# Two attention layers and two linear-attention layers on one core: 27 normalised rows to GpSimd, more PSUM homes, a new order

## The chip, the core and the metric

The kernel runs on one core of a Trainium2 chip. It uses TensorE (matmul; PE in the profile), VectorE (DVE), ScalarE (ACT), GpSimd (POOL) and the queues of SyncE (SP) and ScalarE for transfers. The metric is the device time of one execution in microseconds, as the median of several runs.

## The reference

The input X has 2048 rows (tokens) of 512 numbers, in bfloat16. Four blocks follow each other, A, B, A, B, and each adds its result to X:

```
x = x + A(layernorm(x))
x = x + B(layernorm(x))
x = x + A(layernorm(x))
x = x + B(layernorm(x))
layernorm(x) = (x - mean) / sqrt(var + 1e-5)      # per row
```

A is attention with 32 heads of 16 numbers in four segments of 512 tokens. Within a segment it is causal softmax attention. From the second segment on a memory is added: the sum of phi(k) v over the earlier segments, read with phi(q), with phi(t) = t + 1 above zero and exp(t) below. A gate per head mixes the two. B is linear attention without a mask: q and k go through a small matrix per head, a softmax of the result and one of its negative make the features, the sum of features of k times v is taken over all tokens, and q reads it. Both end with a projection.

## The kernel before

X stays in SBUF as 16 tiles of 128 tokens. A chunk is four tiles, which is also a segment of A. The work of the two layers (L = 0 and 1, each one A and one B) is cut into steps. A step is what one engine does without a wait in between, and it belongs to one of these families (names as in the code, line of the profile behind them):

- **ln** (lines 790 to 825) normalises a chunk: per tile `stats` (L801) and `aggr` (L802) on VectorE, `veps` (L811) and `pow` (L813) for 1/sqrt, then `xn` (L817): (X - mean) times 1/sqrt, one tile of 128 x 512 in bfloat16, 64 of them in the program, all on VectorE. Two tiles make a pair, which one DMA transposition (L585) on SP's queue turns into `xA`, `EQ` or `xB`. Some tiles stand alone; those are turned by TensorE (L601) and copied out of PSUM by VectorE or ScalarE.
- **a_proj** makes k, q and v of a segment. Results come in a PSUM bank and are copied out (L579, tiles `ktok`, `QT`, `VT`); `lo` (L907, L908) is a shifted copy of half a tile of `xA`, `kp` (L938, L939) a copy of parts of K.
- **a_att** does the attention. A unit is two score steps, one on each half of TensorE's rows, each with 1024 columns in two PSUM banks (a *score pair* of banks, kind `st`). ScalarE takes the exponential of such a pair in one instruction (`exp`, L1104, 288 of them), into a tile `PT`. Units on the diagonal are masked: `mask.odd` (L1110) on VectorE or GpSimd, `mask.even` (L1113) on GpSimd. Then TensorE multiplies with v (`pv`, into one bank), and VectorE divides (`r1` L1138, `norm` L1139).
- **a_mem**, **a_state** hold the memory; **a_out** projects, and `resid` (L1165) or `resid.act` (L579, tile `X`) adds to X.
- **b_keys** takes exponentials (L1200), sums them (`bk.half` L1207 on GpSimd, `bk.sum` L1209), inverts (L1218), writes a column of `Vt` (`bk.z`, L1220 to L1222) and the scaled v (L1228). **b_queries** and **b_out** read the sum. `bq.wide` (L1304) widens a 128 x 32 tile on ScalarE or GpSimd.

The order of all this is not made by loops. The program lists 3416 steps with their dependences; four tables at the head of the file then say how they run (`replay`, line 353):

- `ORDER` lists the steps in one sequence. Each engine's queue is its part of that sequence. A number over 10000 marks a score step whose matmuls are issued alternately with those of the step before it (67 of them), so that both halves of TensorE's rows work at once. A negative number is a filler: so many matmuls on a tile of zeros (L1431) where TensorE would have nothing to do (33 fillers with 129 matmuls).
- `ENGINE` has one letter for each step that several engines may run (568 of them), in the order of their creation.
- `SLOTS` gives each tile its buffer, and each PSUM result its bank or banks, as a place in the list of its kind.
- `AFTER` lists pairs of steps (126), the first of which also waits for the second. All 126 are a GpSimd step that waits for a VectorE step.

The kinds of PSUM results and their banks, at line 664:

```
"st": [(0, 1), (2, 3), (4, 5)],
"pv": [(7,), (6,), (5,), (4,)],
"gen": [(7,), (6,), (5,), (4,)],
```

`gen` is a single bank, for projections and the like (289 results), `st` a score pair (288), `pv` the product with v (72). A step of a kind that may run on VectorE or GpSimd is made by `either` (line 575).

Of the kernel before, what the change touches and what calls it, by code (L numbers as in the profile page):

```python
# [8 lines left out]
ALU = mybir.AluOpType  # L9
# [266 lines left out]
class Program:  # L276
# [22 lines left out]
    def R(self, *key):  # L299
        r = self.fixed.get(key)  # L300
        if r is None:
            r = self.fixed[key] = Res()
        return r
# [236 lines left out]
class Kernel:  # L540
# [249 lines left out]
    def ln(self, c, pris, groups=((0, 1), (2, 3)), by_pe=(), pool=None, by_act=False):  # L790

        R = self.R
# [683 lines left out]
```

## Time and profile before

| | |
|---|---|
| median of 3 runs | 478.36 us (478.14 to 478.48) |
| profiled execution | 478.63 us |
| span of its trace | 476.9 us |
| granted TensorE clock | 1.00 |
| HBM read, written | 6.32 MB, 2.10 MB |

The span is from the first to the last instruction of the profiled execution; the 1.7 us between it and that execution's time lie outside it. Busy times are the union of an engine's instructions. PE is TensorE's matmuls, whose ends are modelled; PEld is its weight loads. A row of a group reads: line, engine, operation, tile written <- tiles read, shapes, count | busy us, mean ns of one | idle us of the engine just before them and who ended it.

### The profile page before, as it was taken

The numbers are of one execution on the slowest core, as the hardware profiler recorded it, in microseconds if no ns is written. First come the engines' busy times: TensorE is split into PE (matmuls) and PEld (weight loads), VectorE is DVE, ScalarE is ACT, GpSimd is POOL, SyncE is SP. The second block draws the span as 40 slices with busy tenths as digits, with TensorE's granted clock in tenths as the row PEclk, the third lists the DMA queues.
The fourth block names the chain that finished last, engine by engine and source line by source line (L and its number), as shares of the span: only waits on it lengthen the run. The fifth ranks groups of instructions, "written<-read, shape, count | busy, mean of one in ns | idle before, by whom it ended". The sixth has DMA issues, their size and how long they took to land.

```text
span 476.9 us, 19206 instructions
## 1 busy us (share of the span) xinstructions
PE 465.2 (98%) x8309; PEld 319.3 (67%) x8309; DVE 424.0 (89%) x1008; ACT 429.7 (90%) x666; POOL 268.9 (56%) x435
## 2 busy tenths in 40 slices
PE   7999999999999999999999999999999999999997
PEld 6786677567756567557687666766765666665763
DVE  6999899989998988688999999999998888978885
ACT  3989999999999999986799899989999999999742
POOL 3686758656756685510267575784677578761100
DMA  8679661342422132320346417155434121313366
GB/s 264 115 202 147 144 92 25 69 69 47 48 46 47 25 65 51 36 55 4 67 62 97 74 21 134 25 75 83 59 63 63 25 47 33 51 38 58 70 128 186
DMA packets 115091, 35.86 MB, mean 75 GB/s; under 512 B 106816, under 2 KB 115008, under 8 KB 115008
## 3 DMA queue, kind: packets, MB, share of 16 engines
q1 hardware_dynamic: 112608, 32.54, 38.3%
q10 hardware_dynamic: 2400, 2.11, 1.4%
q8 instruction: 65, 1.06, 0.9%
q14 instruction: 18, 0.15, 0.1%
HBM read 6.32 MB, written 2.10 MB: 18 GB/s over the span
## 4 chain that ended last, share of the span: by engine, by line
PE 59%; DVE 18%; ACT 17%; DMA 3%; POOL 2%; issue 1%; POOLq 0%; DVEq 0%
PE PS L520 57%; ACT PT L1104 12%; DVE D L1110 2%; DVE stats L801 2%; DVE Vt L1228 2%; ACT Ek L1200 2%; DVE xn L817 1%; PE PS L601 1%; DMA EQ<-xn 1%; PE PS L1431 1%; DMA OT<-O 1%; DVE O L1139 1%; ACT K L1285 1%; DVE X L1165 1%; DVE Zk L1209 1%
## 5 line engine op out<-in xcount | busy, mean ns | idle before, releaser
L1104 ACT ACTIVATE PT<-PS 128x1024 bf16<-128x1024 f32 x288 | 284.6, 1083 | 7.8 <-PE PS L520 7.5
L1110 POOL TENSOR_TENSOR D<-PT,modd 128x256 bf16<-128x256 bf16 x133 | 91.6, 699 | 54.2 <-ACT PT L1104 39.1
L1113 POOL TENSOR_SCALAR_AFFINE_SELECT PT<-PT 128x512 bf16<-128x512 bf16 x128 | 83.9, 664 | 30.8 <-DVE D L1110 27.4
L520 PEld LDWEIGHTS PS<-VT,PT 128*128 128x128 bf16 x2048 | 75.0, 96 | 19.2 <-POOL PT L1113 2.5
L520 PE MATMUL PS<-VT,PT 128*128 128x17 bf16 x2048 | 82.4, 171 | 0.7 <-POOL PT L1113 0.2
L520 PE MATMUL PS<-QT,K 32*128 32x64 bf16 (+2 forms) x2176 | 77.9, 213 | 0.3
L520 PE MATMUL PS<-VT,D 128*128 128x17 bf16 x512 | 59.9, 170 | 0.0
L520 PEld LDWEIGHTS PS<-QT,K 32*128 32x128 bf16 x2176 | 41.5, 93 | 20.6 <-ACT PT L1104 10.5
L1110 DVE TENSOR_TENSOR D<-PT,modd 128x256 bf16<-128x256 bf16 x123 | 42.9, 362 | 2.9 <-ACT PT L1104 1.5
L520 PEld LDWEIGHTS PS<-VT,D 128*128 128x128 bf16 x512 | 43.2, 96 | 0.0
L1228 DVE TENSOR_TENSOR Vt<-PS,Zk 128x1024 bf16<-128x1024 f32 (+1 forms) x34 | 39.0, 1158 | 2.0 <-PE PS L520 1.0
L801 DVE BATCH_NORM_STATS2 stats<-X 128x6 f32<-128x512 bf16 x56 | 37.3, 681 | 2.5 <-DMA X<-in_A_x_dram 2.2
L1200 ACT ACTIVATE Ek<-PS 128x512 bf16<-128x512 f32 x64 | 37.6, 664 | 0.9 <-PE PS L520 0.9
L520 PE MATMUL PS<-WA_v,xA 128*128 128x256 bf16 x256 | 36.6, 273 | 0.1
L520 PE MATMUL PS<-WA_k,xA 128*128 128x256 bf16 x256 | 36.3, 273 | 0.2 <-POOL xA L907 0.2
L520 PE MATMUL PS<-xA,WA_q 128*128 128x128 bf16 x512 | 35.7, 219 | 0.5 <-DVE MS L986 0.2
L1165 DVE TENSOR_TENSOR X<-X,PS 128x512 bf16<-128x512 bf16 x50 | 33.7, 679 | 2.2 <-PE PS L520 1.8
L1207 POOL TENSOR_TENSOR Vt<-Ek 128x512 f32<-128x512 bf16 x24 | 27.9, 1164 | 12.9 <-ACT Ek L1200 10.4
L520 PEld LDWEIGHTS PS<-xA,WA_q 128*128 128x128 bf16 x512 | 29.8, 98 | 4.6 <-issue 0.6
L520 PE MATMUL PS<-WA_o,OT 128*128 128x512 bf16 x128 | 32.0, 380 | 0.6 <-DMA OT<-O 0.4
L520 PE MATMUL PS<-WB_o,OT 128*128 128x512 bf16 x128 | 32.1, 379 | 0.1
L1304 POOL COPY O<-rho 128x512 bf16<-128x512 bf16 x24 | 14.9, 634 | 26.5 <-DVE rho L1297 23.3
(157 smaller groups left out, 980.7 us busy)
## 6 DMA issues: line engine op xcount, KB each, us to landing
X<-in_A_x_dram SPq DMA_DIRECT2D x3, 512.0 KB, 9.9
EQ<-in_B_wqkv_dram SPq DMA_DIRECT2D x2, 512.0 KB, 5.4
out_dram<-X SPq DMA_DIRECT2D x8, 128.0 KB, 2.0
out_dram<-X ACTq DMA_DIRECT2D x8, 128.0 KB, 1.9
OT<-O SPq DMA_TRANSPOSE x42, 3.2
WB_v<-in_B_wqkv_dram SPq DMA_DIRECT2D x1, 512.0 KB, 4.3
WA_o<-in_A_wo_dram SPq DMA_DIRECT2D x1, 512.0 KB, 6.5
WB_o<-in_B_wo_dram SPq DMA_DIRECT2D x1, 512.0 KB, 4.7
```

The lines of the kernel that those rows point to most:

```text
L520: return e.matmul(o, l, r, start=st, stop=sp, tile_position=(basep(l), basep(o)))
L601: ins = e.transpose(self.bank(gen).bitcast(BF16)[:, dt * 128:(dt + 1) * 128], src()[:, dt * 128:(dt + 1) * 128], self.ident[:])
L801: self.dve(lambda e, t=t, src=src: e.bn_stats(self.stats[:, t, :], src()), 0.603, [held() if held else R("X", t)], [R("stats", t)], name=" ...
L817: self.dve(lambda e, t=t, n=n, xn=xn: e.tensor_scalar(xn.ap[:, n], self.X[:, t, :], self.mv[:, t, 0:1], self.rstd[:, t:t + 1], op0=ALU.sub ...
L1104: self.act(lambda e, st=st, pt=pt: e.activation(pt.ap[:].rearrange("p b c -> p (b c)"), self.ps[:, st.slot[0] * 512:st.slot[0] * 512 + 102 ...
L1110: self.either(lambda e, d=d, k=k, pt=pt: e.tensor_tensor(d.ap[:, :, k, :].rearrange("p b (z c) -> p b z c", z=2), self.ends(pt.ap[:, :, 25 ...
L1113: self.pool(lambda e, q=quarters: e.affine_select(q(), q(), [[0, 4], [1, 128]], ALU.is_ge, 0.0, base=0, channel_multiplier=-1), 0.6, [pt() ...
L1165: self.dve(lambda e: e.tensor_tensor(X[:, t, :], X[:, t, :], self.bank(gen), ALU.add), 0.6, [R("X", t), gen()], [R("X", t)], name="resid")
L1200: self.act(lambda e, sgn=sgn, Ek=Ek, gen=gen: e.activation(Ek.ap[:, sgn, :], self.bank(gen), ACT.Exp, scale=1.0 - 2.0 * sgn), 512, [gen()] ...
L1207: self.pool(lambda e, Ek=Ek, sums=sums: e.tensor_tensor(sums(), *(Ek.ap[:].rearrange("p s (h j) -> p s h j", h=H)[:, :, :, 8 * k:8 * k + 8 ...
L1228: self.dve(lambda e, w=w, n=n, Vt=Vt, Zk=Zk, gen2=gen2: e.tensor_tensor(self.signed(Vt)[:, w, :, 0:16], self.bank(gen2).rearrange("p (h d) ...
L1304: P.add(("act", "pool"), {"act": lambda e, dst=dst, src=src: e.activation(dst(), src(), ACT.Copy), "pool": lambda e, dst=dst, src=src: e.t ...
```

## The change

Three edits, and new tables.

1. `xn` is made by `either`, so that each of the 64 rows has a letter in `ENGINE` (632 letters).
2. Score pairs may also lie in banks 6 and 7, and single results (`gen`) also in banks 3 and 2.
3. `ORDER`, `AFTER`, `ENGINE` and `SLOTS` are new throughout.

```diff
@@ -31,179 +31,181 @@
 ORDER = (
...
 )
 AFTER = (
-    (389, 128), (164, 47), (181, 51), (353, 38), (371, 144), (201, 191), (212, 152), (202, 192), (213, 175), (1142, 370), (260, 43), (261, 154),
...
+    (91, 88), (169, 351), (341, 1140), (77, 1138), (389, 112), (170, 746), (353, 50), (186, 51), (165, 1139), (197, 196), (1142, 192), (213, 212),
...
 )
@@ -663,9 +665,9 @@
         self.PS.kinds = {
-            "st": [(0, 1), (2, 3), (4, 5)],
+            "st": [(0, 1), (2, 3), (4, 5), (6, 7)],
             "pv": [(7,), (6,), (5,), (4,)],
-            "gen": [(7,), (6,), (5,), (4,)],
+            "gen": [(7,), (6,), (5,), (4,), (3,), (2,)],
             "two": [(6, 7), (4, 5), (0, 1), (2, 3)],
             "wide": [(7,), (6,), (4,), (5,), (0,), (1,), (2,), (3,)],
         }
@@ -814,9 +816,9 @@
             xn = self.p_xn.tile()
             for n, t in enumerate(4 * c + i for i in grp):
-                self.dve(lambda e, t=t, n=n, xn=xn: e.tensor_scalar(xn.ap[:, n], self.X[:, t, :], self.mv[:, t, 0:1], self.rstd[:, t:t + 1],
-                                                                    op0=ALU.subtract, op1=ALU.mult), 0.324,
-                         [R("X", t), R("mv", t), R("rstd", t)], [xn(n)], port=True, name="xn")
+                self.either(lambda e, t=t, n=n, xn=xn: e.tensor_scalar(xn.ap[:, n], self.X[:, t, :], self.mv[:, t, 0:1], self.rstd[:, t:t + 1],
+                                                                       op0=ALU.subtract, op1=ALU.mult), 0.324, 0.63,
+                            [R("X", t), R("mv", t), R("rstd", t)], [xn(n)], name="xn")
```

The tables, read out step by step, say the following. Counts of steps per engine that differ:

| step | VectorE | ScalarE | GpSimd |
|---|---|---|---|
| xn | 64 to 37 | | 0 to 27 |
| mask.odd | 123 to 126 | | 133 to 130 |
| copy of k (`ktok`) | 10 to 15 | 18 to 13 | |
| copy of v (`VT`) | 15 to 16 | 17 to 16 | |
| resid.act (`X`) | 2 to 4 | 6 to 4 of those that may move | |
| turned rows (`xA`) | 3 to 5 | 5 to 3 | |
| kp | 13 to 15 | 2 to 3 | 17 to 14 |
| lo | 11 to 10 | 6 to 6 | 15 to 16 |
| bk.z | 7 to 6 | 4 to 9 | 21 to 17 |
| bq.wide | | 8 to 6 | 24 to 26 |
| folded weight (`WB`) | 7 to 6 | 1 to 2 | |
| turned output (`OT`) | 7 to 6 | 5 to 6 | |

The rows moved to GpSimd belong to 20 pairs and 2 tiles that stand alone: in 15 pairs one row of the two moves, in 5 both. Score steps that are issued alternately with the one before go from 67 to 75, fillers from 33 with 129 matmuls to 36 with 143, entries of AFTER from 126 to 142, each again a GpSimd step that waits for a VectorE step. Stores from ScalarE's queue go from 8 to 7, from SP's from 8 to 9.

| PSUM results | banks 0/1 | 2/3 | 4/5 | 6/7 |
|---|---|---|---|---|
| score pairs (288) | 132 to 132 | 137 to 97 | 19 to 33 | 0 to 26 |
| single results `gen` (289) | 0 | 0 to 68 | 128 to 109 | 161 to 112 |

More of the change, by code (lines that the diff above doesn't have):

```diff
@@ L33 @@
 ORDER = (
[137 rows of a table removed]
[137 rows of a table added]
 )
 AFTER = (
[12 rows of a table removed]
[14 rows of a table added]
 )
 ENGINE = (
-    "daddaadadaadadapaapapadaadaapppddppddpdpdpddpdpdpppppdppddpdpapadpadadpdpdapapaddaddddddppppapapppdppdpdddddppdpdddpdppppdddpppddpddadpaadad"
-    "daaddadddpdapdpppappdpdddddpppdpppdddddddppdpddddppddpddpapaapadaadaddapdpdddpppppppdppddppdddddddddddppdppddddddpddpdpppddadappdpappadaaaaa"
-    "aaaaaadaaapdapdadpaddddddpadaapppppdpdddppddddpdppppdpdppdpddpdadddpdpadaaaadpapadpdppapppddppppppddddpppdddppppppdppddpppppdddapaapaaaapddd"
-    "apapaadpappppppdddddddppdpddpddddppppdppppddddpppdddddddaddaadpaddapddadppppppdpdppppddddpdppdddpdpppddddddpdpppddpddaddpdaapapaasasassasaaa"
@@ L191 @@
-    "aassdads"
+    "dddaddddaaddpdapadapaapddaaaadaadpdpppdpddddddddpdpdppppddppppdpppddpadadpapadpdaddpapaadadddddadddppappapppddpppdpppdppddddddddddppppppdddd"
+    "pppddpdppdddaaadddddpaaddddadpdppapppppppdpppddpdppddpdpddpdddppdddddpdppdddpdpppapaadadaapadddpddaddddddadppppppddpddpppddddddpdddppdpppddd"
+    "dppdpdppdddadddddapddpapppaddaaaadpadadddddaaapaapdaaaaddddaddddaadddpdpppdpdddddddpppppddddppddppdpppdaaddpddadpapadaapddpddpadppapapdppppp"
+    "ppddddpppdddpddpdpdpppdppppddddpdpaapaapapaaddpaaadpdadpdppppappppppdpdpddppdddddddddpddpppdppdppdpdddpppppddddddpdddddadpdddddpddpdaapppppd"
@@ L192 @@
+    "pppppppddpdppddddpdpdppddddppdddddpddadppdddpaappapaasaasssassassasadaaa"
 )
 SLOTS = (
-    "00001102030001020030111201203100120141131150261033007081111329031012001000001131231051221312013312002300037180012120111134021610039001002130"
-    "01301102006021210004019120120031231700001313001120208101100011002711900231111104062201100210203305170010310221130013100381901022313032110310"
-    "00611111004022202331120212233150810310330312020700210328190100113105100210013320710109030231118000012015013000221710100121300113410112503711"
@@ L197 @@
-    "02000131800100202110123003261901201312103415013100021170111220023360211232800913010031310120022170009111051038001011000309011223100037021110"
-    "22025081100302001137190111100003031516031002020021201320040381113112001322130351200161012220133000112323319012303101107120221121214003518000"
-    "10230209031200102001061030271013120411100301052193686272072110202112210012430006121012023333123245167302013210120314500040153201305112300161"
-    "07025123011123210110311001214710050002241011500023203160311110128091001200030710032235022110111124061003011313230028101022101139100021224102"
@@ L201 @@
-    "71001123061101231210021002901113034081031200110310410160212311013017081021010121011000235061213031090101220213000001210310303041002001332210"
-    "35061121322700110238100324130190101001120122210103303001104120171001121001121309100131011030002103204110022117081111200300012011229110020103"
-    "24100300611112280030029131000110212101050710122026101119001310003211713221801112142021035012133222718033119101021314002231112017100503081090"
-    "01113270302024013210518011011000210406110321110700102313203103212109041210320601110001703123213100230301519022112330122218033061123210123506"
@@ L205 @@
-    "13210239011020070113182300001002214130200311501611200122321031023711110008954301673041113200050231103211074036521000721210010314300013412512"
-    "1130101130043156211207122130021306451"
+    "00100102034050000001111220011304100213115061207021030101458092510210102103001023105121112200133413001210819300231031002121060112030137102110"
+    "00213020040233106003107120300041520328000411010022005119000114021708211330104261110200221010230042135370115403103101201200381901230123200103"
+    "10401211126102002311021210233519012133003071020231003081900010021031050213201170110381023021309113110110170100201801132103205111100003113023"
@@ new lines @@
+    "26010401518310040353432030709352302011120304036111103308110122011002122003270110233115091122312073480501330341001010051220801217210900113011"
+    "02102304103025121080911030013341521307320305320433202035250631113011002102113120030271203311101042159240010312400082530100212232150103061201"
+    "01320204091300102301170000228103201051021104126379201121180211030412252502430110030252412330323241506172010223110024534005011670046512172300"
+    "11057221102602214032115030243400103213518020131306073063201110273901504000350381120002111340110023100602333103321221712020910113022105301032"
@@ new lines @@
+    "28112103206132011001103390202421550720100415000100220152205601101117280532001411022050030425014150921021010405010023230610201032101415230134"
+    "15000221133370200812022333111090111201011211006032023321003110017120310100619013111010110030000221300310012021270810100031201200390120421510"
+    "03260130211011035002318101122203413020709130112201050200301110140100923120812000136072120024235110222310432140524829015010223046251100301427"
+    "01022261801102110131171902001210102131021001003380310112202405103600111100113200100302801202024130210023212017160321131251903340601321320207"
@@ L207 @@
+    "10132200600121801303200642930243045200111320040121073035200431250832211069232210140451210250021432211040573031206300401321102216203000227311"
+    "1023622020320041115330211152617405162"
 )
```

298 rows, old and new, of tables (AFTER, ORDER) are left out of this document.

## The prediction

> **What bounds the kernel now.** I read the head of the page first (busy shares, then the chain that ended last), then the busy time by windows, then the groups by line of each engine.
>
> ```profile
> span 476.9 us, 19206 instructions
> PE 465.2 (98%) x8309; PEld 319.3 (67%) x8309; DVE 424.0 (89%) x1008; ACT 429.7 (90%) x666; POOL 268.9 (56%) x435
> PE 59%; DVE 18%; ACT 17%; DMA 3%; POOL 2%; issue 1%; POOLq 0%; DVEq 0%
> PE PS L520 57%; ACT PT L1104 12%; DVE D L1110 2%; DVE stats L801 2%; DVE Vt L1228 2%; ACT Ek L1200 2%; DVE xn L817 1%; PE PS L601 1%; DMA EQ<-xn 1%; PE PS L1431 1%; DMA OT<-O 1%; DVE O L1139 1%; ACT K L1285 1%; DVE X L1165 1%; DVE Zk L1209 1%
> ```
>
> Four engines work side by side. PE reads 98%, but its matmul ends are modelled, and its weight loads fill only 67%, so 98% does not say that TensorE is out of room. VectorE is idle for 476.9 - 424.0 = 52.9 us of the span and ScalarE for 476.9 - 429.7 = 47.2 us. GpSimd has 208 us left. The chain passes to VectorE for 18% and to ScalarE for 17% of the span.
>
> The windows (cut where the chain changes engine) say where the spare time lies. Columns: window; PE, PEld, VectorE, ScalarE, GpSimd busy.
>
> ```profile
> 62.00:94.00 32.00, 30.59 (x608) 21.92 (x600) 30.81 (x74) 31.26 (x43) 22.20 (x36) 1.00 0.38 60
> 200.00:243.00 43.00, 42.41 (x510) 29.12 (x508) 38.67 (x82) 33.93 (x82) 7.18 (x14) 1.00 0.25 38
> 311.00:400.00 89.00, 88.46 (x1750) 60.05 (x1746) 82.75 (x196) 86.39 (x114) 61.49 (x94) 1.00 0.38 59
> 439.00:477.00 38.00, 34.43 (x330) 22.69 (x327) 27.86 (x49) 19.12 (x61) 2.62 (x5) 1.00 0.53 125
> ```
>
> Where attention runs, ScalarE is busy for 31.26 of 32 us and 86.39 of 89 us, VectorE for 30.81 and 82.75. Of ScalarE's 47.2 idle us, 9.1 lie around the change of layers (200 to 243) and 18.9 in the last 38 us, where no attention runs. So in the attention stages both are close to full, and GpSimd is the only engine with room. The clock is 1.00 throughout and plays no part.
>
> TensorE's loads for the score matmuls show who is late:
>
> ```profile
> L520 PEld LDWEIGHTS PS<-QT,K 32*128 32x128 bf16 x2176 | 41.5, 93 | 20.6 <-ACT PT L1104 10.5 <-issue 3.4 <-ACT Ek L1200 0.8
> L520 PEld LDWEIGHTS PS<-QT,KP 32*128 32x128 bf16 x512 | 16.5, 92 | 17.5 <-ACT PT L1104 7.6 <-issue 2.3 <-ACT Ek L1200 1.3
> L520 PEld LDWEIGHTS PS<-VT,PT 128*128 128x128 bf16 x2048 | 75.0, 96 | 19.2 <-POOL PT L1113 2.5 <-issue 2.3 <-ACT PT L1104 1.9
> ```
>
> The first two groups waited 10.5 + 7.6 = 18.1 us for an exponential to free its two PSUM banks; the third, which loads the finished probabilities, only 2.5 for a mask by GpSimd. I take these waits as a sign that ScalarE is the pacemaker, more than that banks are short: with ScalarE at 97%, a third home would only let scores queue up earlier.
>
> **The change part by part.** The engine table, read beside the list of steps that may run on several engines, gives all moves. First VectorE's prices (busy us and mean ns after the bar):
>
> ```profile
> L817 DVE TENSOR_SCALAR xn<-X,mv,rstd 128x512 bf16<-128x512 bf16 x64 | 26.3, 427 | 3.5 <-ACT rstd L808 2.3 <-POOL rstd L813 0.6
> L1110 DVE TENSOR_TENSOR D<-PT,modd 128x256 bf16<-128x256 bf16 x123 | 42.9, 362 | 2.9 <-ACT PT L1104 1.5 <-PE PS L520 1.1
> L579 DVE CAST ktok<-PS 128x512 bf16<-128x512 f32 x10 | 6.7, 674 | 0.1
> L579 DVE CAST VT<-PS 128x512 bf16<-128x512 f32 x15 | 10.3, 686 | 0.2
> L579 DVE CAST X<-PS 128x512 bf16<-128x512 f32 x2 | 1.4, 688 | 0.3 <-PE PS L520 0.3
> L579 DVE COPY xA<-PS 128x512 bf16<-128x512 bf16 x3 | 1.3, 417 | 0.3 <-PE PS L601 0.3
> L938 DVE COPY KP<-K 128x512 bf16<-128x512 bf16 x13 | 4.1, 319 | 0.0
> ```
>
> 27 rows leave: 27 x 26.3/64 = 11.1 us. In come, net: 3 odd masks (3 x 0.35 = 1.0), 5 copies of k (3.4), 1 of v (0.7), 2 of X (1.4), 2 turned rows xA (0.8), 2 of KP (0.6), together 7.9. Four small ones leave (a shifted half, a column of Vt, a folded weight, a turned output; 0.3 to 0.7 each by the sizes above, about 1.8). **VectorE: -11.1 + 7.9 - 1.8 = -5.0 us.**
>
> ScalarE:
>
> ```profile
> L579 ACT ACTIVATE ktok<-PS 128x512 bf16<-128x512 f32 x18 | 11.8, 654 | 0.3 <-PE PS L520 0.3
> L579 ACT ACTIVATE VT<-PS 128x512 bf16<-128x512 f32 x17 | 10.9, 670 | 0.0
> L579 ACT ACTIVATE X<-PS 128x512 bf16<-128x512 f32 x12 | 7.2, 603 | 6.9 <-PE PS L520 5.4 <-DVE X L1165 1.4
> L1304 ACT ACTIVATE O<-rho 128x512 bf16<-128x512 bf16 x8 | 5.0, 624 | 0.5 <-DVE rho L1297 0.5
> L579 ACT ACTIVATE xA<-PS 128x512 bf16<-128x512 bf16 x5 | 3.0, 596 | 1.3 <-PE PS L601 1.3
> L1220 ACT ACTIVATE Vt<-Zk 128x64 bf16<-128x64 f32 x4 | 2.0, 511 | 0.0
> L939 ACT ACTIVATE KP<-K 128x512 bf16<-128x512 bf16 x2 | 1.4, 700 | 0.0
> ```
>
> Out, net: 5 x 0.654 + 0.670 + 2 x 0.603 + 2 x 0.596 + 2 x 0.624 = 7.6. In: 5 columns of Vt (5 x 0.511), a KP (0.70), a folded weight and a turned output (0.60 each, as xA) = 4.5. **ScalarE: -3.1 us.** So the room that the rows leave on VectorE is partly spent on ScalarE's copies.
>
> GpSimd has no such row in this trace. Its nearest:
>
> ```profile
> L1110 POOL TENSOR_TENSOR D<-PT,modd 128x256 bf16<-128x256 bf16 x133 | 91.6, 699 | 54.2 <-ACT PT L1104 39.1 <-PE PS L520 5.7 <-DVE QT L579 4.0
> L1113 POOL TENSOR_SCALAR_AFFINE_SELECT PT<-PT 128x512 bf16<-128x512 bf16 x128 | 83.9, 664 | 30.8 <-DVE D L1110 27.4 <-DVE VT L737 0.4 <-DVE PhiQ L960 0.4
> L1304 POOL COPY O<-rho 128x512 bf16<-128x512 bf16 x24 | 14.9, 634 | 26.5 <-DVE rho L1297 23.3 <-DMA OT<-O 3.1
> L938 POOL COPY KP<-K 128x512 bf16<-128x512 bf16 x17 | 11.1, 652 | 5.2 <-ACT K L921 2.1 <-DMA K<-ktok 2.1 <-DVE K L922 0.9
> L1222 POOL CAST Vt<-Zk 128x64 bf16<-128x64 f32 x21 | 10.3, 489 | 12.0 <-ACT Zk L1216 10.1 <-DVE Zk L1218 1.8
> L1149 POOL TENSOR_TENSOR O<-O,AM 128x512 bf16<-128x512 bf16 x1 | 1.2, 1152 | 0.1
> ```
>
> A row has one streamed input of 512 elements, like the copies (634, 652) and the selection (664), and unlike the sum of two inputs (1152). Bounds 0.49 to 1.15; I take 0.64, by the three rows with its form. 27 x 0.64 = 17.3; 2 widenings and a shifted half more (1.7), 3 masks, 3 KP and 4 columns of Vt fewer (6.0): **GpSimd +13.0 us**, 269 to 282, at 59% still the emptiest.
>
> A row issues nothing itself; its pair's transposition on SP's queue waits for both rows. 15 pairs get one row from each engine, 5 pairs both from GpSimd, 2 rows stand alone. In a mixed pair the rows run beside each other: about 0.64 instead of 0.41 + 0.41, so not later. In the other five it is 1.28 for 0.82, 0.5 late; a transposition behind such a pair on SP's queue is late with it. At 5 x 0.5 + 2 x 0.23 = 3.0 us in all, and with VectorE's rows only 1% of the chain, I cost it at nothing; if all of it fell on the chain it would cost 3.0. Table AFTER grows from 126 to 142 entries, each a GpSimd step waiting for a VectorE step. Behind such a step on GpSimd stand masks, and for them TensorE's loads of the probabilities. GpSimd's spare time covers it now; without that cover the 2.5 us that these loads wait for a mask would grow, at most double.
>
> Next, **the port**. VectorE's steps that read and write SBUF are longer in some cases:
>
> ```profile
> L817 DVE TENSOR_SCALAR xn<-X,mv,rstd x64: 315/408/795, 5.5 to 436.8; 128x512 bf16<-128x512 bf16 x64
> L1110 DVE TENSOR_TENSOR D<-PT,modd x123: 224/286/802, 22.0 to 425.7; 128x256 bf16<-128x256 bf16 x123
> ```
>
> The same shape takes 795 instead of 408 ns at worst, a hit of about 0.39. The masks' mean of 362 against their median of 286 makes 123 x 0.076 = 9.3 us of lengthening beside 269 us of GpSimd. With 13 us more in proportion, +0.5; I take +1 for the other steps with such a form. So VectorE's net is -4.0.
>
> The Trainium skill, "SBUF — State Buffer", section "Who interferes with whom", says that GpSimd and a VectorE instruction that uses both its ports, or has two SBUF inputs, exclude each other, and the one that comes second blocks for the whole instruction. The spread of these two rows agrees. By that rule each moved row can block VectorE, which would turn the gain round; that is the third rival.
>
> **TensorE.** The matmuls stay. Steps of a score pair whose two halves are issued alternately rise from 67 to 75 (the marks over 10000 in ORDER). The timeline of TensorE prices it, and a piece of the chain in order of time prices a filler:
>
> ```profile
> 243.34 0.21 PE L520 MATMUL PS<-QT,KP 32*128 32x64 bf16 x4
> ...
> 243.69 1.05 PE L520 MATMUL PS<-WA_k,xA 128*128 128x256 bf16 x8
> 244.66 0.20 PE L520 MATMUL PS<-QT,KP 32*128 32x64 bf16 x2
> ...
> 245.00 0.61 PE L520 MATMUL PS<-WA_v,xA 128*128 128x256 bf16 x4
> ```
>
> ```profile
> 168.56 0.63 PE PS L1431 x6
> ```
>
> Both halves alternated took 243.69 - 243.34 = 0.35 us, one half alone 245.00 - 244.66 = 0.34. So each new pairing saves about 0.33: 8 x 0.33 = 2.6 us, of which 59% on the chain, -1.5. Fillers (warm matmuls where TensorE would stand idle) go from 129 to 143; they fill idle time and cost nothing, at most 14 x 0.63/6 = 1.5.
>
> **Banks.** By the slot table, score steps in banks 0/1, 2/3, 4/5, 6/7 go from 132, 137, 19, 0 to 132, 97, 33, 26, and 68 of 289 single results go to banks 2 and 3. That gives scores other homes and takes homes from them; bounds -6 (a third of the 18.1 us of waits) to +6 (as much again). I take 0: no bank is added, and ScalarE paces.
>
> **Sum.** If an engine keeps its idle time, the span is its load plus that. VectorE: 424.0 - 4.0 + 52.9 = 472.9. ScalarE: 429.7 - 3.1 + 47.2 = 473.8, the later. Less 1.5 from TensorE: 472.3. The profiled execution took 478.63, 1.7 over its span: 474.0. It lies 0.3 above the median of 478.36: **473.7**.
>
> **The rivals.**
> Banks free the scores: a third of the 18.1 us goes as well, 473.7 - 6 = 468. For it: 18.1 us is the largest wait of TensorE for one step. Against: ScalarE has hardly idle time in those stages to give back.
>
> Nothing to measure: the new order loses about what the moves win, 478.4. For it: 59% of the chain is TensorE's, whose work stays. Against: both loads fall.
>
> Slower, by the port: each moved row blocks a VectorE step. Place: attention stages such as 62 to 94, where VectorE has 1.2 us free in 32. Price: the hit of 0.39 seen above on up to 27 rows, 10.5 us, or 0.25 on the mean, 6.8. VectorE's load is then 424.0 - 5.0 + 6.8 to 10.5 = 425.8 to 429.5, the span 478.7 to 482.4, the time 480.1 to 483.8: about 482. It decides from 5.0/27 = 0.19 us of blocking per row. For it: hits exist. Against: the lengthening so far is small beside GpSimd's 269 us.
>
> That the change does not do what it says is excluded by the tables: 27 rows carry GpSimd's letter.
>
> **How the numbers follow.** The forecast (471 to 477.4) 0.45, banks 0.15, nothing 0.12, port 0.28. A measurement of this kernel tells about 0.2%, 1 us, from no change. Faster 0.45 + 0.15 = 0.60, same 0.12, slower 0.28. The range 467 to 482.5 leaves out the far half of the bank and port cases, under 2 in 10. The forecast's own range is 471 to 477.4.
>
> **What would show it.** Right: a GpSimd group of 27 at the row's line, of about 0.64 us each; VectorE near 420 and ScalarE near 426.6 busy with idle times near 53 and 47; score loads still waiting for exponentials. Wrong: rows near 1.15 on GpSimd, or VectorE near 428 with longer means of masks and copies (port); score waits for ScalarE well under 12 us (banks); or the loads down as said but idle times grown, so that order, not load, sets the time.

## The result and the profile after

The changed kernel takes 507.22 us (median of 4 runs, 502.74 to 509.73) against 478.42 before: ratio 1.0588, interval 1.0511 to 1.0664. It is 28.8 us slower. The forecast was 473.7 us with a range of 467 to 482.5, and faster. Times are medians; of e14 below one execution of six took 808.88 us, and its ratio leaves that one out.

The head of the page, the clock's row of its slices (tenths of full speed) and the chain:

```profile
span 506.0 us, 19213 instructions
...
PE 469.7 (93%) x8260; PEld 324.8 (64%) x8323; DVE 425.9 (84%) x992; ACT 429.8 (85%) x662; POOL 321.2 (63%) x455
...
PEclk9989879988999999999998999999997999989999
...
PE 42%; ACT 22%; DVE 16%; POOL 10%; DMA 6%; issue 3%; ACTq 0%; POOLq 0%; DVEq 0%
PE PS L522 40%; ACT PT L1106 14%; POOL xn L819 4%; ACT Ek L1202 3%; POOL PT L1115 2%; DMA EQ<-xn 2%; DVE stats L803 2%; DMA xB<-xn 2%; DVE D L1112 2%; POOL D L1112 2%; DVE Vt L1230 1%; DMA X<-in_A_x_dram 1%; PE PS L1433 1%; DVE O L1141 1%; DVE AM L1011 1%
```

VectorE (424.0 before) and ScalarE (429.7) carry what they carried. Only GpSimd's load rose, from 268.9 to 321.2 us, and with 63% it is still the least loaded engine. Yet GpSimd is now on the chain for 10% instead of 2%, and its rows `xn` (line 819 in the changed kernel) for 4%, some 20 us. The page's slices now have a row for the clock; before, the clock was full throughout.

The row's line, with minimum, median and maximum in ns:

```profile
L819 DVE TENSOR_SCALAR xn<-X,mv,rstd x37: 362/411/846, 5.4 to 465.8; 128x512 bf16<-128x512 bf16 x37
L819 POOL TENSOR_SCALAR xn<-X,mv,rstd x27: 2070/2090/2494, 19.3 to 451.9; 128x512 bf16<-128x512 bf16 x27
```

A row takes GpSimd 2.09 us, five times VectorE's 0.41 and more than three times the 0.64 of the forecast. GpSimd's timeline (start, us, what) shows one of them at work, and TensorE's what waited behind it:

```profile
63.71 2.20 POOL L819 TENSOR_SCALAR xn<-X,mv,rstd 128x512 bf16<-128x512 bf16 x1
65.88 0.67 POOL L1112 TENSOR_TENSOR D<-PT,modd 128x256 bf16<-128x256 bf16 x1
66.52 0.23 POOL L813 TENSOR_SCALAR rstd<-mv 128x2 f32<-128x2 f32 x1
66.71 0.67 POOL L1112 TENSOR_TENSOR D<-PT,modd 128x256 bf16<-128x256 bf16 x1
67.33 0.71 POOL L815 TENSOR_TENSOR rstd<-rstd,negh 128x2 f32<-128x2 f32 x1
68.00 0.64 POOL L1115 TENSOR_SCALAR_AFFINE_SELECT PT<-PT 128x512 bf16<-128x512 bf16 x1
```

```profile
68.79 0.37 PE L522 MATMUL PS<-VT,PT 128*128 128x17 bf16 x9 [1.28 <-POOL PT L1115]
```

The row does not hold up its own reader here. It holds up what stands behind it in GpSimd's queue: masks of D, two steps of 1/sqrt, masks of PT, and with them TensorE, which waits 1.28 us for a masked tile and at 69.76 once more 0.47. Over the whole kernel the loads of the probabilities waited 7.9 us for a mask by GpSimd, where it was 2.5 before:

```profile
L522 PEld LDWEIGHTS PS<-VT,PT 128*128 128x128 bf16 x2048 | 76.1, 97 | 28.0 <-POOL PT L1115 7.9 <-issue 3.7 <-ACT PT L1106 1.4
```

Windows of 5 us around this place and two others (window; PE, PEld, VectorE, ScalarE, GpSimd busy; clock):

```profile
20.00:25.00 5.00, 2.68 (x36) 2.30 (x34) 2.48 (x9) 3.63 (x7) 5.00 (x5) 1.00 0.42 85
25.00:30.00 5.00, 4.91 (x66) 3.64 (x64) 4.92 (x16) 2.34 (x4) 2.85 (x6) 0.66 0.66 155
65.00:70.00 5.00, 2.97 (x81) 2.08 (x77) 3.93 (x11) 4.97 (x8) 4.87 (x8) 0.98 0.73 69
70.00:75.00 5.00, 4.77 (x79) 4.07 (x80) 4.13 (x12) 2.60 (x3) 2.94 (x4) 0.50 0.43 68
110.00:115.00 5.00, 3.37 (x31) 1.23 (x29) 2.06 (x6) 2.86 (x4) 0.61 (x1) 0.57 0.20 37
```

Where GpSimd is full (5.00 and 4.87 of 5 us), TensorE is busy for only 2.68 and 2.97, and in the window behind it the clock is 0.66 and 0.50. So a late row is paid for twice: TensorE stands still, and then runs at half clock for a while.

In the third window GpSimd is nearly idle, and the clock is 0.57. There it is the row's own reader that is late. The pair has one row on each engine. VectorE's row was done at 104.51 + 0.73 = 105.24, GpSimd's at 104.33 + 2.09 = 106.42, and only then did SP issue the transposition, 1.3 us after VectorE's half was ready; it landed at 111.5, and TensorE waited 1.63 us for it:

```profile
104.33 2.09 POOL L819 TENSOR_SCALAR xn<-X,mv,rstd 128x512 bf16<-128x512 bf16 x1 [0.18 <-ACT PT L1106]
...
104.51 0.73 DVE L819 TENSOR_SCALAR xn<-X,mv,rstd 128x512 bf16<-128x512 bf16 x1
...
106.50 1.23 SPq L587 DMA_TRANSPOSE EQ<-xn  x1
...
111.91 0.63 PE L522 MATMUL PS<-WB_k,EQ 128*128 128x512 bf16 x1 [1.63 <-DMA EQ<-xn]
```

Another pair of this kind does the same at 441.6: TensorE waits 1.7 us for its transposition `xB`, and a stretch at half clock follows.

### The profile page after: what moved, and what is told of

It reads as the page before. It is cut to its first block, busy times and chain, and to the rows that moved or that the text cites. A ratio compares the mean times of both kernels' runs of the same rounds, so it can differ in the third digit from the quotient of the medians.

```text
span 506.0 us, 19213 instructions
## 1 busy us (share of the span) xinstructions
PE 469.7 (93%) x8260; PEld 324.8 (64%) x8323; DVE 425.9 (84%) x992; ACT 429.8 (85%) x662; POOL 321.2 (63%) x455
## 4 chain that ended last, share of the span: by engine, by line
PE 42%; ACT 22%; DVE 16%; POOL 10%; DMA 6%; issue 3%; ACTq 0%; POOLq 0%; DVEq 0%
PE PS L522 40%; ACT PT L1106 14%; POOL xn L819 4%; ACT Ek L1202 3%; POOL PT L1115 2%; DMA EQ<-xn 2%; DVE stats L803 2%; DMA xB<-xn 2%; DVE D L1112 2%; POOL D L1112 2%; DVE Vt L1230 1%; DMA X<-in_A_x_dram 1%; PE PS L1433 1%; DVE O L1141 1%; DVE AM L1011 1%
## 5 line engine op out<-in xcount | busy, mean ns | idle before, releaser
L1112 POOL TENSOR_TENSOR D<-PT,modd 128x256 bf16<-128x256 bf16 x130 | 88.2, 688 | 36.7 <-ACT PT L1106 24.9
L522 PEld LDWEIGHTS PS<-VT,PT 128*128 128x128 bf16 x2048 | 76.1, 97 | 28.0 <-POOL PT L1115 7.9
L819 POOL TENSOR_SCALAR xn<-X,mv,rstd 128x512 bf16<-128x512 bf16 x27 | 57.7, 2138 | 17.3 <-ACT rstd L810 15.6
L1112 DVE TENSOR_TENSOR D<-PT,modd 128x256 bf16<-128x256 bf16 x126 | 44.1, 368 | 4.1 <-ACT PT L1106 2.9
L522 PE MATMUL PS<-WA_v,xA 128*128 128x256 bf16 x256 | 39.5, 286 | 1.2 <-DVE D L1112 0.6
L522 PE MATMUL PS<-WA_k,xA 128*128 128x256 bf16 x256 | 38.6, 285 | 2.0 <-POOL xA L909 1.8
L1140 DVE RECIPROCAL r<-PS 128x16 f32<-128x16 f32 (+1 forms) x72 | 16.7, 235 | 17.6 <-PE PS L522 17.6
## 6 DMA issues: line engine op xcount, KB each, us to landing
X<-in_A_x_dram SPq DMA_DIRECT2D x3, 512.0 KB, 11.4
```

The source lines that it names most:

```text
L522: return e.matmul(o, l, r, start=st, stop=sp, tile_position=(basep(l), basep(o)))
L819: self.either(lambda e, t=t, n=n, xn=xn: e.tensor_scalar(xn.ap[:, n], self.X[:, t, :], self.mv[:, t, 0:1], self.rstd[:, t:t + 1], op0=ALU. ...
L1112: self.either(lambda e, d=d, k=k, pt=pt: e.tensor_tensor(d.ap[:, :, k, :].rearrange("p b (z c) -> p b z c", z=2), self.ends(pt.ap[:, :, 25 ...
L1140: self.dve(lambda e, r1=r1, view=view, nt=nt: e.reciprocal(r1.ap[:, 0:nt, :], view()[:, :, :, 16]), 0.07 + 0.0475 * nt, [pv()], [r1()], na ...
```

## The experiments

Theory P: the price of the row on GpSimd is the loss. Rival O: the new order and banks lose by themselves. Rival L (the forecast's third): GpSimd and VectorE block each other at the port, and the row is long only for that.

**e1: the rows back on VectorE.** In ENGINE of the changed kernel the 27 letters of the rows are `d`; all else as changed.

> The changed kernel with its own order, banks and waits, but the 27 rows made by VectorE again. Theory P (the price: a row costs GpSimd 2.1 us instead of 0.64): the loss goes, 474 to 483 us, clock 1.00; VectorE carries 11 us more than the order was made for, so perhaps a little over the kernel before. Theory O (the new order and banks lose by themselves): 495 us or more, score waits as in the changed kernel.

484.71 us, ratio 1.0129 (1.0112 to 1.0146), clock 1.00. So 22.5 of the 28.8 us hang on who makes the rows, and 6.3 stay. The time is 1.7 us over P's range and far under O's.

**e2: GpSimd's rows as copies.**

```diff
-    e.tensor_scalar(xn.ap[:, n], self.X[:, t, :], self.mv[:, t, 0:1], self.rstd[:, t:t + 1], op0=ALU.subtract, op1=ALU.mult)  # GpSimd's
+    e.tensor_copy(xn.ap[:, n], self.X[:, t, :])  # GpSimd's
```

> The changed kernel, but GpSimd's 27 rows are plain copies of X, so those rows are left without their normalisation; order, banks and waits as changed. It gives the row the price that the forecast took for it. Theory P: row 0.6 to 0.65 us, time 471 to 477.4 us, as forecast, clock 1.00. Theory O: 490 us or more in spite of the short rows.

478.29 us, ratio 1.0000 (0.9982 to 1.0018). The busy times of its page, and from its groups the loads of the score matmuls and the rows:

```profile
PE 457.0 (95%) x8260; PEld 318.8 (66%) x8323; DVE 422.2 (88%) x992; ACT 428.4 (89%) x662; POOL 280.8 (58%) x455
```

```profile
L522 PEld LDWEIGHTS PS<-QT,K 32*128 32x128 bf16 x2176 | 40.2, 93 | 22.2 <-ACT PT L1108 10.8 <-issue 3.4 <-ACT Ek L1204 1.2
...
L821 POOL COPY xn<-X 128x512 bf16<-128x512 bf16 x27 | 17.0, 632 | 16.6 <-ACT rstd L810 13.3 <-DVE Zk L1213 2.1 <-DVE stats L803 0.2
...
L522 PEld LDWEIGHTS PS<-QT,KP 32*128 32x128 bf16 x512 | 16.4, 92 | 17.9 <-ACT PT L1108 8.0 <-issue 2.4 <-DVE QT L581 1.3
```

With rows of 0.63 us the whole loss is gone: 507.2 - 478.3 = 28.9 us is what the row's length costs in this order. P holds against O. But the gain does not appear either: the same time as before, where the forecast said 473.7 for just this price. Beside e1 one sees why the sum is nothing: in the new order the 27 rows, taken off VectorE at this price, bring 484.7 - 478.3 = 6.4 us, and with the rows left on VectorE the new order, banks and letters cost 6.3. (The page is of an execution of 481.96 us, the longest of ten.) And the scores wait 10.8 + 8.0 = 18.8 us for exponentials, as before (18.1), in spite of the new homes.

**e3: the rows alone.** The kernel before, its order and banks, and the same 27 letters `p`.

> The kernel before with its own order and banks, and only the same 27 rows made by GpSimd. Theory P: a row 2.1 us, the time rises by 15 to 35 us to 493 to 513, clock under 0.99. Theory O: within 3 us of 478.4.

513.27 us, ratio 1.0721 (1.0669 to 1.0772), clock 0.963.

```profile
L817 POOL TENSOR_SCALAR xn<-X,mv,rstd 128x512 bf16<-128x512 bf16 x27 | 59.7, 2212 | 13.9 <-ACT rstd L808 12.9
```

The rows alone lose 34.7 us, just over the top of P's range: the new tables do not make the loss; with them it is some 6 us smaller.

**e4: forms of one instruction**, X to another tile, GpSimd alone and beside VectorE.

> No part of the computation, it writes zeros: forms of one instruction on 128x512 bfloat16 by GpSimd alone (copy, two scalars from SBUF with two operations, one of each, the same with constants, narrower tiles, a product of two tiles), then VectorE's forms alone, beside GpSimd's rows, beside its copies, and statistics beside rows. Theory P: the row's form takes 2.1 us alone, so its length is its own; which of scalar source, second operation or width makes it is open. Theory L (the shared port): the row takes 0.6 to 0.7 us alone and 2 us only beside VectorE. For VectorE beside GpSimd's rows, L expects single hits up to the row's length, P hits under 0.5 us.

Groups of its page: 25 is the row's form, 28 the copy, 30 one operation with a scalar from SBUF, 31 one with a constant, 32 two with constants, 33 and 34 the row's form at 256 and 128 columns, 35 a product of two tiles.

```profile
L25 POOL TENSOR_SCALAR g<-X,sc 128x512 bf16<-128x512 bf16 x15 | 31.8, 2131 | 0.5 <-DVE v L40 0.3
L28 POOL COPY g<-X 128x512 bf16<-128x512 bf16 x21 | 13.6, 696 | 8.4 <-DVE v L40 8.3
...
L32 POOL TENSOR_SCALAR g<-X 128x512 bf16<-128x512 bf16 x3 | 5.7, 1925 | 0.0
L30 POOL TENSOR_SCALAR g<-X,sc 128x512 bf16<-128x512 bf16 x3 | 4.6, 1562 | 0.0
L31 POOL TENSOR_SCALAR g<-X 128x512 bf16<-128x512 bf16 x3 | 4.4, 1489 | 0.0
L33 POOL TENSOR_SCALAR g<-X,sc 128x256 bf16<-128x256 bf16 x3 | 3.6, 1218 | 0.0
L35 POOL TENSOR_TENSOR g<-X,Y 128x512 bf16<-128x512 bf16 x3 | 3.4, 1151 | 0.0
L34 POOL TENSOR_SCALAR g<-X,sc 128x128 bf16<-128x128 bf16 x3 | 2.4, 795 | 0.0
```

The timeline of GpSimd gives the copy (8.73), the row (10.51) and the product (37.30) alone, and the row beside VectorE (40.77); that of VectorE gives six rows, products and copies alone (3.33 to 7.28), and six rows beside GpSimd's rows (40.78) and beside its copies (54.02):

```profile
8.73 1.73 POOL L28 COPY g<-X 128x512 bf16<-128x512 bf16 x3 [8.30 <-DVE v L40]
10.51 6.19 POOL L25 TENSOR_SCALAR g<-X,sc 128x512 bf16<-128x512 bf16 x3
...
37.30 3.37 POOL L35 TENSOR_TENSOR g<-X,Y 128x512 bf16<-128x512 bf16 x3
40.77 13.21 POOL L25 TENSOR_SCALAR g<-X,sc 128x512 bf16<-128x512 bf16 x6
```

```profile
3.33 2.03 DVE L25 TENSOR_SCALAR v<-X,sc 128x512 bf16<-128x512 bf16 x6 [2.21 <-DMA Y<-in_A_x_dram]
5.27 2.10 DVE L39 TENSOR_TENSOR v<-X,Y 128x512 bf16<-128x512 bf16 x6
7.28 1.30 DVE L40 COPY v<-X 128x512 bf16<-128x512 bf16 x6
40.78 3.11 DVE L25 TENSOR_SCALAR v<-X,sc 128x512 bf16<-128x512 bf16 x6 [32.19 <-POOL g L35]
...
54.02 3.86 DVE L25 TENSOR_SCALAR v<-X,sc 128x512 bf16<-128x512 bf16 x6 [6.09 <-POOL g L25]
```

Alone the row takes 6.19/3 = 2.06 us. L falls: the length is its own. It is the kind of instruction: with one operation and a constant it is 1.49, far over the copy; the second operation adds 0.4 to 0.5 us, scalars from SBUF some 0.1. It grows by (2.06 - 0.80)/384 = 3.3 ns per column. No narrower tile (0.80 us for a quarter of the columns) or cheaper scalar brings it near the copy. On VectorE six rows take 1.1 us longer beside GpSimd's rows: they do hinder each other, by 0.18 us per VectorE row.

**e5: rows as copies in the old order.** e3 with e2's copies.

> The order and banks of the kernel before, and the same 27 rows by GpSimd as plain copies (those rows left without normalisation): the forecast's row price, without the new order and banks. Row about 0.63 us. Theory L (loads: VectorE gets 11 us lighter and the span follows in part): 473 to 477 us. Theory N (a load taken from VectorE in an order made for another load turns into idle time; the rows come 0.2 us later): 478 to 482 us.

479.79 us, ratio 1.0026 (1.0008 to 1.0044). Theory N: VectorE is relieved of 27 rows, and the time rises a little.

**e6: more fillers.** The changed kernel; in ORDER 149 fillers at ten places (24 matmuls ahead of the transposition at 22 us, 18 each ahead of those near 270 and 379, and so on).

> The changed kernel with 149 more filler matmuls on zeros, at the ten places where TensorE's queue stood still longest (about as many as fill each gap); rows on GpSimd at full length. Theory K (half of the loss is the clock: seven stretches at half clock, 36 us in all, each behind a gap): clock 0.99 to 1.00 and 490 to 499 us. Theory S (the loss is the standing still itself, and the clock only shows it): clock up, time 504 to 510.

498.97 us, ratio 1.0429 (1.0403 to 1.0456).

```profile
core 0: 497.2 us, clock 1.000
```

This lies in theory K's range, at its edge. Of the 28.9 us, 507.2 - 499.0 = 8.2 came back with the clock. At most it could be (1 - 0.966) x 506 = 17 us, the clock time lost in the trace after; fillers that overran their gaps may hide some of the difference, so I estimate the clock's share at 8 to 17 us. At full clock 499.0 - 478.3 = 20.7 us remain. They are TensorE standing still and what the fillers overran; by the same bounds the standing still is 12 to 20.7.

**e7: rows of middle length.** e2 with `tensor_tensor(X, X, add)` in place of the copy.

> The changed kernel, GpSimd's 27 rows as the sum of X with itself (left without normalisation), a form of 1.15 us, between the copy of 0.63 (478.3 us) and the true row of 2.1 (507.2). Theory linear: 478.3 + 28.9 x (1.15 - 0.63)/(2.14 - 0.63) = 488 us. Theory threshold (the order has room for half a microsecond of lateness, and the clock falls only behind long gaps): 479 to 483 us, clock 1.00.

483.85 us, ratio 1.0119 (1.0081 to 1.0157), clock 1.00.

```profile
L821 POOL TENSOR_TENSOR xn<-X 128x512 bf16<-128x512 bf16 x27 | 28.5, 1056 | 14.8 <-ACT rstd L810 13.3 <-DVE Zk L1213 0.2
...
L819 DVE TENSOR_SCALAR xn<-X,mv,rstd 128x512 bf16<-128x512 bf16 x37 | 20.1, 551 | 1.8 <-POOL rstd L815 1.5
```

Neither expectation fits as it stands. With the clock set apart, rows longer by 0.42 us (27 x 0.42 = 11.4 us) cost 483.9 - 478.3 = 5.6, 49%, and rows longer by 1.5 us at full clock (27 x 1.5 = 40.5) cost 12 to 20.7, 29 to 51%. So up to half of every microsecond of lateness reached the end, no threshold shows, and the low clock came on top. The 49% is not lateness alone: VectorE's own 37 rows took 551 ns on average in e7 and 461 in e2, and its load is 426.0 against 422.2 us. How much of the 5.6 that is was not taken apart.

**e8: twelve rows back** on VectorE: the five pairs that GpSimd made alone, and the two single tiles.

> The changed kernel with 12 of the 27 rows back on VectorE, those of the five pairs that GpSimd made alone and the two single tiles; 15 rows stay on GpSimd, one in each pair. Between all back (484.7 us) and none back (507.2 us). Theory linear in rows: 484.7 + 22.5 x 15/27 = 497 us. Theory pairs (two rows in a row on GpSimd make the pair 4.2 us late and break the clock): under 491 us, clock 0.99 or more.

497.74 us, ratio 1.0394 (1.0374 to 1.0414), clock 0.986: linear in the rows (497 expected), and not under 491. 12 of 27 rows (44%) brought back 9.5 of 22.5 us (42%), so the rows of pairs that GpSimd made alone show no extra cost.

**e9, e10, e11: lighter loads in the old order.** The kernel before, with

```diff
-    exp over self.ps[:, b * 512:b * 512 + 1024]          # e9, e11
+    exp over self.ps[:, b * 512:b * 512 + 1008]          # full width at the first use of a buffer
-    e.bn_stats(self.stats[:, t, :], src())               # e10, e11
+    e.bn_stats(self.stats[:, t, :], src()[:, 0:448])
```

> The kernel before, each exponential over 1008 of its 1024 columns (the last 16 keep older values): 288 x 16 x 0.83 ns = 3.8 us less for ScalarE, nothing else changed. Theory L (the sum of the forecast: an engine keeps its idle time, ScalarE paces): 474.2 to 475.5 us. Theory N (in an order made for another load, what is taken from one engine mostly turns into idle time): 477.3 to 479.

> The kernel before, the row statistics over 448 of 512 columns (the result differs a little): 64 x 64 x 1.04 ns = 4.3 us less for VectorE. Theory L: ScalarE paces, so 477.5 to 478.6 us; if VectorE paces, 474 to 475. Theory N: 477 to 479.

> Both of the above in one kernel: ScalarE 3.8 us and VectorE 4.3 us lighter, about the net relief that the forecast gave the changed kernel (3.1 and 4.0), in the order and banks of before. Theory L: 474 to 475.5 us; then the missing gain of the changed kernel with short rows was eaten by its new order. Theory N: 476.5 to 478.5; then the forecast's sum was wrong by itself.

e9 476.48 us, ratio 0.9953 (0.9938 to 0.9968). e10 478.23, 0.9988 (0.9972 to 1.0004). e11 475.99, 0.9943 (0.9926 to 0.9961). The loads, e9 then e10:

```profile
PE 464.5 (98%) x8309; PEld 319.6 (67%) x8309; DVE 423.0 (89%) x1008; ACT 426.8 (90%) x666; POOL 267.9 (56%) x435
```

```profile
PE 465.1 (98%) x8309; PEld 319.7 (67%) x8309; DVE 420.9 (88%) x1008; ACT 429.5 (90%) x666; POOL 267.6 (56%) x435
```

ScalarE's load fell by 2.9 us and the time by 2.2: three quarters pay. VectorE's fell by 3.1 and the time by 0.4, which is not clear of nothing. Both together (e11) bring 2.7, the sum of the two; e9 and e11 lie between their two expectations. So in the old order ScalarE is the pacemaker, as read from the waits, and VectorE's relief is worth next to nothing. The new order, made without these rows on VectorE, looks otherwise: there e1 and e2 differ by 5.8 us in VectorE's load (428.0 and 422.2) and by 6.4 in time.

The loads fell by less than the prices said (3.8 and 4.3); why was not taken apart. For instructions that move whole, one reason is in the timeline of the kernel before: the next instruction can start before the last has ended, so the mean length of an instruction is more than what it adds to the load. This copy of k lasts 0.78 us, but the next instruction starts 0.48 us after it:

```profile
385.22 0.78 ACT L579 ACTIVATE ktok<-PS 128x512 bf16<-128x512 f32 x1
385.70 0.79 ACT L1285 ACTIVATE K<-PS 128x512 bf16<-128x512 f32 x1
```

**e12: the other moves alone.** The kernel before, its order, all rows on VectorE, the other letters of ENGINE as changed.

> The kernel before with its own order, banks and waits, all rows on VectorE, and only the other engine letters of the change (copies of k and others from ScalarE to VectorE and so on): VectorE +6.1, ScalarE -3.1 us. Theory L: VectorE's load plus its idle time, 484.7 us, if VectorE paces, or 475.5 if ScalarE does. Theory N: 479 to 483; the steps change their engine in an order that was not made for it, and both waits and loads grow a little.

501.44 us, ratio 1.0472 (1.0446 to 1.0498), far over both expectations; the clock was 0.986. Waits that grew most:

```profile
ACT PT L1104 <- PE PS L520: 22.4, 32, 2.6
...
POOL rstd L811 <- DVE mv L802: 22.1, 15, 7.4
```

Before they were 7.5 and 9.2 us. So this set of letters does not fit the old order. Which of the 205 moved steps cost most was not tried.

**e13: five copies alone.** The kernel before, only the five copies of k from ScalarE to VectorE.

> The kernel before, only the five copies of k that the change moves go from ScalarE to VectorE; result complete. ScalarE -3.3 us, VectorE +3.4. By what e9 and e10 measured (ScalarE's relief pays 57%, VectorE's 10%): -1.9 + 0.3 = -1.5, so 477 us, faster than both kernels. Theory N (a step that changes engine without a new order waits at its new place): 479 to 484 us.

479.02 us, ratio 1.0011 (1.0002 to 1.0020). No gain: by the shares of e9 and e10 it should have been 1.5 us faster. Its page has ScalarE's load lower by only 1.3 us (428.4) and VectorE's higher by 1.2 (425.2), not 3.3 and 3.4, so by the loads the gain was at most 1 us; why even that is missing was not taken apart. Of the versions that leave nothing out, none was faster than the kernel before.

**e14: no pairing.** The marks over 10000 taken from ORDER of the kernel before.

> The kernel before with none of its 67 score steps issued alternately with the one before; same steps, order and banks. By the forecast's price, 67 x 0.33 = 22 us of TensorE, 59% of it on the chain: 491.5 us. If TensorE's queue has room behind the exponentials: under 484.

480.11 us, ratio 1.0031 (1.0019 to 1.0043). All 67 pairings together are worth 1.5 us.

**e15: no table AFTER.** e2 with `AFTER = ()`.

> The changed kernel with GpSimd's rows as copies (478.3 us, rows left without normalisation), and the table AFTER empty, so GpSimd starts as soon as its data is there. If the 142 waits cost what they hold back: 475 to 477.5. If they keep GpSimd from holding the port against VectorE: 479 to 484, masks and copies on VectorE longer. Nothing: within 1 us.

479.67 us, ratio 1.0031 (1.0016 to 1.0045) against e2's 1.0000 (0.9982 to 1.0018). The waits cost nothing; they seem to pay about 1 us, but the two intervals touch.

## Why the prediction was wrong

1. **The row's price on GpSimd is the step that failed.** "A row has one streamed input of 512 elements, like the copies", 0.64 us with bounds 0.49 to 1.15. It was 2.09 (median) to 2.14 (mean), outside the bounds, and GpSimd's load rose by 52.3 us instead of 13.0. No row of the trace before had a plain TENSOR_SCALAR by GpSimd on a wide tile; the form was judged by its streams, and e4 shows that the operation decides. The change with the row as short as forecast (e2) is 28.9 us faster: the whole loss.

2. **Lateness was costed at nothing because GpSimd had room.** The room was there: 63% busy after the change. But each step behind a row in GpSimd's queue is as late as the row, and up to half of it reached the end (e7, e6). The waits of the loads for a mask, bounded at twice 2.5 us, became 7.9. And "in a mixed pair the rows run beside each other ... so not later" holds at 0.64 us and fails at 2.09: each of the 15 mixed pairs is then 2.09 - 0.82 = 1.27 us late, and TensorE stood still behind two of their transpositions (at 110 and 447 us). The forecast's own count, 3.0 us in all, becomes 15 x 1.27 + 5 x 3.36 + 2 x 1.68 = 39 us of lateness. So this step hangs on the first.

3. **The clock was left out**, since it was 1.00 throughout. In the changed kernel, with TensorE's longer gaps, the low clock cost an estimated 8 to 17 us (e6, the trace).

4. **The sum "load plus idle time" was too generous.** With the row at 0.64 it gave 473.7; e2 measured 478.3. VectorE's relief, 4.0 in the forecast, was 1.8 in e2's load, ScalarE's 1.3 instead of 3.1: the moves were priced at mean lengths, though instructions overlap, which explains a part. And the sum has no term for the new tables themselves. By e1 they cost 6.3 us with the rows on VectorE, and by e2 the rows' move gives 6.4 back, so that the two cancel. Whether the 6.3 are the order, the banks, the other letters, or only that this order was made for rows on GpSimd, is open. In the old order the same move costs 1.2 us even with the rows as copies (e5).

5. **Pairing**: 1.5 us for 8 pairs were forecast; 67 are worth 1.5 (e14), so 8 some 0.2. The price 0.33 of a pairing was TensorE's own time, and little of it reaches the end; that TensorE mostly has it to spare behind ScalarE is argued, not shown.

6. **Right**: ScalarE as pacemaker of the kernel before, with the waits of the scores as its sign (e9); that the new homes would not shorten these waits (18.8 against 18.1 us in e2), though what the banks are worth alone was not tried; the waits of AFTER at no cost (e15).

7. **The port rival** named the sign and about 482, by another mechanism. The effect exists (0.18 us per VectorE row in e4, 0.30 beside copies), but e2, with GpSimd's copies beside VectorE, loses nothing: it is not what made 507. Its sign stayed out too: VectorE's masks took 368 ns on average in the changed kernel and 362 before.

```profile
L1112 DVE TENSOR_TENSOR D<-PT,modd 128x256 bf16<-128x256 bf16 x126 | 44.1, 368 | 4.1 <-ACT PT L1106 2.9 <-PE PS L522 1.1
```

What stays open: how much the new order and banks give or cost apart from each other. Banks alone were not tried. Why e12's letters cost 23 us was not taken apart.

## What to carry to other kernels

Before work is handed to an idle engine, take the duration of that very operation on that engine, not of one with the same streams: an engine that copies at VectorE's half speed made this one at a fifth. Price a longer step by what stands behind it in its in-order queue: an engine with 40% of its time free gave up to half of each late microsecond to the end. Count the row's reader as well: a pair made by two engines is ready with the slower one. A mean length is not what an instruction adds to its engine's load, where instructions overlap. A table of engines and an order made for one price can't be judged apart; a copy in place of the disputed step (e2) tells price and order apart in one run.

## What the runs showed of the hardware that was not expected

GpSimd's operations with scalars: 1.49 us for 128x512 bfloat16 with one operation and a constant, 2.06 for the row's form, against 1.73/3 = 0.58 for a copy and 3.37/3 = 1.12 for a product of two tiles (e4, alone).

The Trainium skill, "GPSIMD Engine Reference", section "Engine selection", calls GpSimd roughly line-rate for one input and half of VectorE's speed for two. In e4 VectorE takes 1.30/6 = 0.22 us for the copy, 2.10/6 = 0.35 for the product and 2.03/6 = 0.34 for the row, so GpSimd is some 2.7, 3.2 and 6 times slower; and its operations with one input and scalars are slower than the product of two. The measurement decides.

Beside GpSimd's copies each VectorE row took 3.86/6 = 0.64 us, about the length of a copy (11.87/18 = 0.66 beside VectorE), as if the two took turns. Beside GpSimd's rows of 2.1 us it took only 0.52, and six of them were through by 43.9 while GpSimd's own six filled 40.8 to 54.0 without a break. The Trainium skill, "SBUF — State Buffer", section "Who interferes with whom", has the second fully block for the whole instruction. The copies agree with that, the long rows do not.

In the changed kernel the clock fell to half behind windows in which TensorE was still busy for 2.7 to 3.0 of 5 us, thus without a long standstill. The longest wait of its matmuls in the changed kernel (us in total, times, longest) is 2.3 us:

```profile
PE PS L603 <- DVE xn L819: 3.1, 2, 2.3
```

The Trainium skill, "TensorE: Matmul & The Clock Gate", Part 1, speaks of an idle window of about 3.4 us. The changed kernel has no wait as long as that, and its clock fell all the same. Only e3 comes near, with one wait of 3.3 us:

```profile
PE PS L520 <- DVE WB_k L579: 3.3, 1, 3.3
```
